# A decode block's tail on one NeuronCore: one strided store, filler matmuls, and waits merged into the matmuls

## The chip, the cores and the metric

The kernel runs on one core of one Trainium2 chip. The metric is the device time in microseconds (us) of one launch. The profile of a run covers the span from the first to the last instruction, which is shorter than the measured time; times of day in the text ("at 650.6") are us from the start of that span.

## The reference

A decode step for 4 sequences: layer norm, query projection, attention over a cache of 4096 keys and values per head, output projection and residual, then a second layer norm and an MLP with the activation h·tanh(softplus(h)).

```python
# x: (4, 1, 640); k_cache, v_cache: (4, 32, 4096, 128); all bf16
q = layernorm(x) @ wq                                   # 32 heads of 128
p = softmax(q . k_cache * 128**-0.5)
h = x + (p . v_cache) @ wo                              # wo: (4096, 640)
y = h + act(layernorm(h) @ w1 + b1) @ w2                # w1: (640, 1728), w2: (1728, 640)
```

The caches are 268 MB of the 283 MB that are read.

## The kernel before

Each engine has its own program, and they meet through semaphores. 16 K tiles and 16 V tiles go through three SBUF slots; VectorE multiplies K by the query, TensorE folds and makes the PV products. Once the last K tile is used up, its slot takes the weights wo and w1, another slot takes w2. All that the change touches is the tail: what TensorE does from the last PV product on.

```python
def need(self, *keys):                 # cut to what matters
    ...
    if sem in self.take:               # semaphores that count from zero again each loop
        self.eng.wait_ge(h, d).then_inc(h, -d)   # a wait instruction of its own, which subtracts
    elif self.live:
        self.eng.wait_ge(h, n)         # can be carried by the next instruction

def pe_tail():                         # cut
    def wo_mm(k):                      # 40 matmuls: weights 128x128 from wo, moving 4 columns
        pe.need(("wo", k), ("a", k))
        for j in range(G):
            for c in range(DC):
                w = wo_sb[:, k, j, :].rearrange("p (m c) -> p c m", c=DC)[:, c, :]  # step 5
                mm(y_ps[:, c, :], w, a_t[:, k, j, :], ...)
    wo_mm(0); o_mm(NT - 1); l_mm(hg); wo_mm(1); a_mm(hg)
    ...                                # two matmuls that clear PSUM
    wo_mm(2); wo_mm(3)
    pe.need("st")                      # sums for the second layer norm, in fp32
    ...
    pe.need("cen")
    for c0, c1 in zip(W1S, W1S[1:]):   # two parts: 42 and 28 matmuls
        pe.need(("w1", c0))
        if c1 == DC:                   # bias, in fp32
            ...
        for j in [FM] + list(range(FM)):
            for c in range(c0, c1):
                w = w1_sb[:, c, 0 : FM * P].rearrange("p (f j) -> p j f", j=FM)[:, j, :]  # step 13
                mm(h1_ps[...], w, cen[:, c, :], ...)
    pe.need("h_lo")                    # adds h: 40 small matmuls
    ...
    pe.need("act")
    def w2_mm(j):                      # 4 matmuls, one per 32-column group; weights act: 4 columns
        for k in range(CG):
            mm(y2_ps[k * QD : k * QD + N, :], act[0:rows, j, :], w2_sb[:, j, cs], ...)

for q in range(CG):                    # SyncE: the result, four rows of 320 B each time
    load(sp, out_rows[:, q * OC : (q + 1) * OC], o_bf[q * QD : q * QD + N, :], ("out", q), "OUT")
```

The softmax here doesn't subtract the row's maximum and nothing guards it: scores larger than these inputs give would overflow.

## Time and profile before

| what | number |
|---|---|
| time, median of 4 runs | 669.49 us (669.01 to 669.72) |
| span of the profiled run | 667.44 us |
| last V tile lands, last PV product starts | 637.07, 637.21 |
| fourth wo load lands | 650.37 |
| w1's first part lands, second part | 653.66, 656.09 |
| w2's three parts land | 658.67, 661.06, 661.86 |

The page of the kernel before gives, in 40 slices, the TensorE clock that was granted and the busy share of the DMA queues, in tenths:

```profile
span 667.4 us, 5166 instructions
...
PEclk9668787879759796869557887878766878788875
DMA  9999999999999999999999999999999999999995
```

The DMA row says that the queues are 90% busy or more in every slice but the last; a change behind the last V tile (637.07) can win or lose only in the last 30 us. The windows of the kernel before show stages of that tail. The columns are the window, its length, then for PE, PEld (weight loads), DVE, ACT and POOL the busy time and the number of instructions, and at the end the granted clock, the DMA share and GB/s:

```profile
642.40:644.10 1.70, 1.70 (x45) 1.68 (x41) 0.00 (x0) 1.56 (x2) 0.00 (x0) 1.00 1.01 422
649.50:650.60 1.10, 0.01 (x1) 0.00 (x0) 0.00 (x0) 0.00 (x0) 0.00 (x0) 0.50 0.96 399
650.60:652.40 1.80, 1.73 (x40) 1.68 (x40) 0.00 (x0) 0.00 (x0) 0.00 (x0) 0.50 0.98 407
654.00:656.50 2.50, 2.50 (x41) 2.48 (x42) 0.57 (x5) 1.58 (x2) 0.00 (x0) 0.50 1.04 370
661.20:663.40 2.20, 2.19 (x56) 1.62 (x56) 0.00 (x0) 0.00 (x0) 0.00 (x0) 0.50 0.00 1
```

The first and third lines are the first and the fourth part of wo: 40 matmuls in the same 1.7 us, once at clock 1.00 and once at 0.50. The second line is TensorE's one long idle stretch behind the last V tile and before the activation chain, 1.1 us. The fourth is w1's first part, the fifth w2. The timeline of the kernel before (start, length, engine, line, operation, out<-in, count, and in brackets the idle time before it) shows the end of the chain:

```profile
650.66 1.73 PE L657 MATMUL y_ps<-a_t,slotB 128*128 128x4 bf16 x40 [1.15 <-PEq L44]
652.66 0.62 PE L657 MATMUL misc<-st,ones_d 128*128 128x20 f32 x2 [0.27 <-DVE st L562]
653.53 0.18 DVE L582 TENSOR_TENSOR cen<-st,mu 128x20 bf16<-128x20 f32 x1
654.00 2.73 PE L657 MATMUL red<-cen,slotB 128*64 128x4 bf16 x42 [0.30 <-PEq L44]
656.59 0.66 PE L657 MATMUL red<-b1s,ident_f 128*128 128x56 f32 x2
657.18 1.93 PE L657 MATMUL red<-cen,slotB 128*64 128x4 bf16 x28
660.69 0.22 DVE L646 SCALAR_TENSOR_TENSOR act<-tb,hm 128x56 bf16<-128x56 f32 x1
661.21 0.30 PE L657 MATMUL red<-w_tail,act 64*4 64x160 bf16 x4 [1.35 <-PEq L44]
663.44 0.32 DVE L653 CAST o_bf<-red 128x160 bf16<-128x160 f32 x1 [2.53 <-PE red L657]
663.79 1.33 SPq L239 DMA_DIRECT2D out_dram<-o_bf  x4
```

Each line waits for the one above it. The fourth wo part waits for its load (the releaser "PEq" is TensorE's own wait instruction, which hides the DMA behind it). The activations are ready at 660.91 and the first w2 matmul starts at 661.21, 0.3 us later. The four stores take 1.33 us to issue.

### The profile page before, as it was taken

How to read it: one execution, taken by the hardware profiler on the slowest of the kernel's cores; microseconds unless marked ns; L12 is line 12 of the kernel's file. 1: busy time of each engine (PE TensorE's matmuls, PEld its weight loads, DVE VectorE, ACT ScalarE, POOL GpSimd, SP SyncE). 2: the span in 40 equal slices, each digit the busy share in tenths (PEclk: the TensorE clock that was granted, in tenths of full speed). 3: DMA queues.
4: the chain of work that ended last, by engine and by line, in shares of the span. 5: the costliest groups of instructions: out<-in, count | busy, mean ns of one | idle time of the engine just before them, and what ended most of it. 6: DMA issues, size and time to landing. Idle time of an engine off the chain costs nothing. (4 is left out here: it accounts for less than half of the span.)

```text
span 667.4 us, 5166 instructions
## 1 busy us (share of the span) xinstructions
PE 394.1 (59%) x2729; PEld 79.4 (12%) x1769; DVE 406.5 (61%) x250; ACT 41.0 (6%) x157; POOL 2.6 (0%) x14
## 2 busy tenths in 40 slices
PE   0855748456327585847308395848426575847576
PEld 0700100101101010101100010100110010010155
DVE  1068988295058788666128798768208798849412
ACT  0200000000000010000000000000000000000011
POOL 1000000000000000000000000000000000000000
PEclk9668787879759796869557887878766878788875
DMA  9999999999999999999999999999999999999995
GB/s 378 437 440 440 433 420 409 441 440 437 429 436 436 436 436 424 424 440 436 432 432 440 436 432 432 416 440 436 433 432 436 440 436 433 428 425 440 428 396 198
DMA packets 6405, 283.55 MB, mean 425 GB/s; under 512 B 948, under 2 KB 1016, under 8 KB 1528
## 3 DMA queue, kind: packets, MB, share of 16 engines
q1 hardware_dynamic: 6160, 283.35, 98.5%
q8 instruction: 10, 0.16, 0.1%
q10 hardware_dynamic: 232, 0.01, 0.0%
q14 instruction: 3, 0.02, 0.0%
HBM read 283.35 MB, written 0.01 MB: 425 GB/s over the span
## 5 line engine op out<-in xcount | busy, mean ns | idle before, releaser
L466 DVE TENSOR_TENSOR slotA<-slotA,q_bc 128x8192 bf16<-128x8192 bf16 x32 | 140.7, 4416 | 110.9 <-DMA slotA<-in_A_k_cache_dram 110.7
L466 DVE TENSOR_TENSOR slotB<-slotB,q_bc 128x8192 bf16<-128x8192 bf16 x32 | 140.7, 4416 | 16.3 <-DMA slotB<-in_A_k_cache_dram 16.3
L667 PE MATMUL red<-slotA,ident 128*128 128x512 bf16 x480 | 141.0, 459 | 0.0
L477 DVE TENSOR_REDUCE s_f<-red 128x64 f32<-128x1024 f32 x64 | 78.1, 1220 | 96.9 <-PE red L667 96.8
L667 PE MATMUL red<-slotB,ident 128*128 128x512 bf16 x480 | 123.3, 415 | 0.0
L657 PE MATMUL red<-slotA,ident 128*128 128x512 bf16 x32 | 14.2, 445 | 119.3 <-PEq L44 119.3
L657 PE MATMUL pv<-slotC,e 128*32 128x512 bf16 x768 | 52.4, 434 | 42.7 <-PEq L44 42.7
L657 PE MATMUL red<-slotB,ident 128*128 128x512 bf16 x32 | 14.1, 441 | 87.0 <-PEq L44 87.0
L348 ACT ACTIVATE ex<-s_f 128x64 bf16<-128x64 f32 x64 | 16.4, 256 | 502.3 <-DVE s_f L477 502.3
L491 DVE TENSOR_TENSOR e<-ex,hmask 128x512 bf16<-128x512 bf16 x64 | 39.8, 682 | 0.0
L657 PEld LDWEIGHTS pv<-slotC,e 128*32 128x32 bf16 x768 | 22.5, 108 | 103.0 <-issue 89.4
L657 PEld LDWEIGHTS red<-slotA,ident 128*128 128x128 bf16 x32 | 3.2, 98 | 200.7 <-issue 200.6
L657 PEld LDWEIGHTS red<-slotB,ident 128*128 128x128 bf16 x32 | 3.2, 98 | 165.1 <-issue 165.1
L657 PEld LDWEIGHTS o_ps<-pv_sb,selo 128*32 128x32 f32 x128 | 12.7, 109 | 59.1 <-issue 59.1
L657 PE MATMUL o_ps<-pv_sb,selo 128*32 128x128 f32 x128 | 17.0, 276 | 0.0
L657 PE MATMUL pv<-slotA,e 128*32 128x512 bf16 x256 | 14.5, 380 | 0.9 <-PEq L44 0.9
L358 ACT COPY pv_sb<-pv 128x512 f32<-128x512 f32 x16 | 9.4, 585 | 75.7 <-PE pv L657 75.7
L348 ACT ACTIVATION_READ_ACCUMULATOR ex<-s_f 128x1 f32 x64 | 11.9, 186 | 0.0
L657 PE MATMUL red<-q_all,sel 32*128 32x128 bf16 x128 | 10.8, 280 | 0.8 <-PEq L44 0.8
L657 PEld LDWEIGHTS red<-q_all,sel 32*128 32x128 bf16 x128 | 10.6, 128 | 1.2 <-issue 1.2
L516 DVE RECIPROCAL rl<-misc 32x1 f32<-32x1 f32 x4 | 0.6, 150 | 16.2 <-PE misc L657 16.2
L657 PEld LDWEIGHTS pv<-slotA,e 128*32 128x32 bf16 x256 | 7.0, 97 | 22.1 <-issue 16.5
(93 smaller groups left out, 74.0 us busy)
## 6 DMA issues: line engine op xcount, KB each, us to landing
slotC<-in_A_wq_dram SPq DMA_DIRECT2D x1, 5120.0 KB, 15.1
slotB<-in_A_wo_dram SPq DMA_DIRECT2D x4, 1280.0 KB, 19.1
slotB<-in_B_w_dram SPq DMA_DIRECT2D x1, 1296.0 KB, 26.8
slotA<-in_B_w_dram SPq DMA_DIRECT2D x1, 960.0 KB, 30.3
slotB<-in_B_w_dram SPq DMA_DIRECT2D x1, 864.0 KB, 28.8
slotA<-in_B_w_dram SPq DMA_DIRECT2D x1, 800.0 KB, 32.0
slotA<-in_B_w_dram SPq DMA_DIRECT2D x1, 320.0 KB, 30.2
slotC<-in_A_v_cache_dram SPq DMA_DIRECT2D x12, 44.9
```

Source lines behind the costliest of these rows:

```text
L348: lambda: a.activation(out=ex[:, sl], in_=s_f[:, sl], func=ACT.Exp, scale=SCALE, accum_out=rs[:, b, s : s + 1],),
L358: lambda: a.copy(out=pv_sb[:, :, :].rearrange("p r d -> p (r d)"), in_=pv[:, :]),
L466: lambda: v.tensor_tensor(out=t, in0=t, in1=q_bc[:, hg, b, :].unsqueeze(1).to_broadcast([P, RS, Dh]), op=ALU.mult,),
L477: lambda: v.tensor_reduce(out=s_f[:, s * RS : (s + 1) * RS], in_=red[:, k : k + 2, :].rearrange("p k (r c) -> p (k r) c", c=CW), axis=AX.X ...
L491: lambda: v.tensor_tensor(out=e[:, sl, :], in0=ex[:, sl].unsqueeze(2).to_broadcast([P, RS, G]), in1=hmask[:, :].unsqueeze(1).to_broadcast( ...
L516: dv.do(lambda: v.reciprocal(out=rl[:, :], in_=l_ps), ("rl", hg), DV)
L657: lambda: nc.tensor.matmul(out_, lhsT=lhsT, rhs=rhs, start=start, stop=stop, skip_group_check=skip),
L667: return t.add_instruction(mybir.InstMatmult(name=nc.get_next_instruction_name(), engine=mybir.EngineType.PE, ins=[t.lower_ap(rhs), t.lowe ...
```

## The change

Its intent: TensorE's clock falls to half in the tail, so fill its gaps with matmuls that compute nothing and keep the clock up; let the first matmul behind a wait carry the wait; give the result in one store instead of four. For the store, the result's 16 rows have to lie at an even step over the partitions, so h and the activations get 32-column weights, 28 of the columns zero, which puts the rows eight partitions apart.

```diff
+    def freeze(self):                       # from here on the taken semaphores are no longer reset
+        self.base = dict(self.seen)
-            if sem in self.take:
+            if sem in self.take and self.base is None:
...
+                low = self.base.get(sem, 0) if sem in self.take else 0
+                self.eng.wait_ge(h, n - low)
...
+    spread = sb("spread", (P, 2 * DC + FC, N, ROW), BF16, tail, topA)   # zeroed; ROW = 8
+    h_hi, h_lo, act = (...)                 # every eighth column of it
...
-        for q in range(CG):
-            load(sp, out_rows[:, q * OC : (q + 1) * OC], o_bf[q * QD : q * QD + N, :], ...)
+        load(sp, out_rows.rearrange("b (k o) -> k b o", k=CG), o_bf[0:P:ROW, :], "out", "OUT")
...
+    def keep_busy(n):                       # fillers: 128x128 weights, 512 moving columns
+        for k in range(n):
+            (mm_same if k else mm)(red[:, 3, :], ident[:, :], slot["C"][:, 0:512], True, True)
...
+        pe.freeze()
         wo_mm(0)
+        keep_busy(4)
         o_mm(NT - 1)
         l_mm(hg)
         wo_mm(1)
+        keep_busy(4)
         a_mm(hg)
...
         wo_mm(2)
+        keep_busy(6)
         wo_mm(3)
...                                          # the norm sums
+        keep_busy(4)
         pe.need("cen")
         for c0, c1 in zip(W1S, W1S[1:]):
-            pe.need(("w1", c0))
             if c1 == DC:
                 ...                          # bias
+                keep_busy(3)
+            pe.need(("w1", c0))
...                                          # h, now with 32-column weights
+        keep_busy(3)
         pe.need("act")
...                                          # w2, now with 32-column weights
+            if j0 == 0:
+                keep_busy(4)
```

More of the change, by code (lines that the diff above doesn't have):

```diff
@@ L27, in restart @@
         self.log = []
+        self.base = None
+    def freeze(self):
+        self.base = dict(self.seen)
     def need(self, *keys):
@@ L45, in need @@
             elif self.live:
-                self.eng.wait_ge(h, n)
+                low = self.base.get(sem, 0) if sem in self.take else 0
+                self.eng.wait_ge(h, n - low)
     def do(self, fn, mark=None, sem=None, by=1):
@@ L192 @@
     b1s = sb("b1s", (P, FC, N), FP32, tail, topA)
-    h_hi = sb("h_hi", (P, DC, N), BF16, tail, topA)
-    h_lo = sb("h_lo", (P, DC, N), BF16, tail, topA)
+    ROW = QD // N
+    spread = sb("spread", (P, 2 * DC + FC, N, ROW), BF16, tail, topA)
+    h_hi, h_lo, act = (
+        spread[:, j0:j1, :, :] for j0, j1 in ((0, DC), (DC, 2 * DC), (2 * DC, 2 * DC + FC))
+    )
     h1 = sb("h1", (P, FC, N), FP32, tail, topA)
@@ L200 @@
     hm2 = sb("hm2", (P, FC, N), FP32, tail, topA)
-    act = sb("act", (P, FC, N), BF16, tail, topA)
     o_bf = sb("o_bf", (P, OC), BF16, tail, topA)
@@ L286, in sync_prog @@
         sp.need("o_bf")
-        for q in range(CG):
-            load(
-                sp, out_rows[:, q * OC : (q + 1) * OC], o_bf[q * QD : q * QD + N, :],
-                ("out", q), "OUT",
-            )
-        sp.need(("out", CG - 1))
+        load(
+            sp, out_rows.rearrange("b (k o) -> k b o", k=CG), o_bf[0:P:ROW, :], "out", "OUT",
+        )
+        sp.need("out")
     def pool_prog():
@@ L311, in pool_prog @@
         po.do(lambda: g.memset(ones_d[:, :], 1.0 / D), "ones_d", "PO")
+        po.do(lambda: g.memset(spread[:, :, :, :], 0.0), "spread", "PO")
         po.do(lambda: g.memset(zeros[:, :], 0.0), "zeros", "PO")
@@ L600, in dve_prog @@
         )
-        dv.do(lambda: v.tensor_copy(out=h_hi[:, :, :], in_=st[:, 0, :, :]), "h_hi", DV)
+        dv.do(lambda: v.tensor_copy(out=h_hi[:, :, :, 0], in_=st[:, 0, :, :]), "h_hi", DV)
         dv.need("std2", "b1b")
@@ L613, in dve_prog @@
             lambda: v.tensor_tensor(
-                out=h_lo[:, :, :], in0=st[:, 0, :, :], in1=h_hi[:, :, :], op=ALU.subtract
+                out=h_lo[:, :, :, 0], in0=st[:, 0, :, :], in1=h_hi[:, :, :, 0], op=ALU.subtract
             ),
@@ L646, in dve_prog @@
             lambda: v.scalar_tensor_tensor(
-                out=act[:, :, :], in0=tb3[:, :, :], scalar=-0.5, in1=hm2[:, :, :],
+                out=act[:, :, :, 0], in0=tb3[:, :, :], scalar=-0.5, in1=hm2[:, :, :],
                 op0=ALU.add, op1=ALU.mult,
@@ L846, in pe_tail @@
                     mm(
-                        y2_ps[k * QD : k * QD + N, :].rearrange("b (m c) -> b c m", c=DC)[:, c, :],
-                        part[:, c, :], ident[:, k * QD : (k + 1) * QD], False, False,
+                        y2_ps[k * QD : (k + 1) * QD, :].rearrange("b (m c) -> b c m", c=DC)[:, c, :],
+                        part[:, c, :, :].rearrange("p n r -> p (n r)"), ident[:, k * QD : (k + 1) * QD], False, False,
                     )
+        keep_busy(3)
         pe.need("act")
@@ L857, in w2_mm @@
                 mm(
-                    y2_ps[k * QD : k * QD + N, :], act[0:rows, j, :],
+                    y2_ps[k * QD : (k + 1) * QD, :],
+                    act[0:rows, j, :, :].rearrange("p n r -> p (n r)"),
                     w2_sb[:, j, cs] if j < FM else w2_tail[0:FT, cs], False, j == FM - 1,
```

## The prediction

> **What bounds the kernel now.** Until the last V tile it streams the caches: the page shows DMA 90% busy or more in all but the last of 40 slices, 425 GB/s. The change touches only what comes after that tile lands (637.0 of a 667.4 us span), so at most 30 us are in play.
>
> In that tail (timeline, windows) TensorE runs without a gap from 637.2 to 649.5: the last PV product 5.2 us, then wo parts of 40 matmuls at 40 ns each, o, l, a. The only real gap is 649.5 to 650.6, for the fourth wo load (landed 650.35). Then a chain: wo part 4 (1.7 us), norm sums, centring (653.7), w1 (60 ns per matmul, to 659.1), activation chain on VectorE (to 660.9), 56 w2 matmuls (661.2 to 663.4, 133 ns per four), copy, four stores issued 0.3 us apart (663.8 to 665.1), the last landing at 666.0, and 1.4 us of fixed end.
>
> **Clock.** The granted clock is 1.00 from 640.5 to 647.4 and 0.50 after. It changes only at steps of 3.41 us, as the Trainium skill, "TensorE: Matmul & The Clock Gate", Part 1, says of its activity window. I counted array work per window (columns times used share of the array): windows at 0.44 of full rate or more stayed fast, those at 0.31 or less fell, and from the slow clock 0.38 was not enough. Is a fast clock worth having? The wo matmuls take 40 ns at 1.00 and at 0.50 alike; the a matmuls take 60 ns at 1.00, as w1's do at 0.50. So wo and w1 are bound by weight loads that do not follow the clock. Only w2 (160 columns at half rate are the 133 ns), the fp32 sums and the bias would gain: about 0.9 + 0.5 us.
>
> **Change, costed.**
> - Store: three issues of 0.3 us leave the chain's end: -0.95 us.
> - Waits: separate wait instructions cost 0.25 us from release to first weight load (act 660.91 to 661.18). Merged: about -0.2 us where still exposed.
> - Fillers: 28 matmuls of 128x512, 0.213 us each fast, 0.427 us slow (the fold matmuls show both), mostly not in gaps. 14 stand before wo part 4, where the gap is 1.1 us. Four beside 3.5 us of small matmuls give about 0.33 of full rate: I expect the clock to fall at 647 to 651 anyway. Then groups 1 to 3 cost 0.9 + 1.3 + 2.6 less the gap: +3.5; the group behind the sums +1.35; behind the bias +1.3; behind h_lo mostly hidden in the 1.9 us activation chain, +0.6; inside w2 +1.7.
> - 32-column padded weights for h and act: w2 stays 133 ns per four; they raise counted activity, so the clock may rise during w2: -0.5 to -1.
>
> Sum: about +6.5 us. If the fillers do hold the clock at 1.00, only about +1.3 us.
>
> **Prediction:** 675.8 us, range 670.5 to 678.5; faster by over 2% 0.01, within 2% 0.97, slower by over 2% 0.02.
>
> **What would show it.** Windows: from the end of the last PV product to wo part 4 grows from 8.3 to 11 to 12.5 us; wo still 40 ns and w1 still 60 ns per matmul at any clock; clock 0.50 over most of w1; one store, landing about 1.1 us after its issue; cen ready over 1 us before the w1 matmuls; TensorE no longer idle before wo part 4.
>
> **What would make it wrong.** Fillers holding the clock at 1.00 (then near 670.6); w1's weight loads following the clock after all, which would save up to 2.5 us and make the change a gain (near 667.5); 32-column weight loads slowing the h products enough to delay w2; another phase of the clock's window.

## The result, and the profile after

| | before | after |
|---|---|---|
| median, 4 runs each | 669.49 us | 675.38 us (674.19 to 675.62) |
| span of the profiled run | 667.44 us | 672.40 us |

The changed kernel is 5.9 us slower; the ratio is 1.0085 with a 95% interval of 1.0068 to 1.0103. Ratios here and below are the mean time of one kernel's fast runs over that of the other's of the same rounds, so not quite the ratio of the medians quoted. The profiled run of the changed kernel is its fastest (674.19), so its profile shows 5.0 us of the loss.

The page of the changed kernel, clock and DMA:

```profile
span 672.4 us, 5177 instructions
...
PEclk9668887879758697968658796868658887879786
DMA  9999999999999999999999999999999999999992
```

The windows of the changed kernel, in the same columns:

```profile
642.50:644.30 1.80, 1.76 (x44) 1.70 (x41) 0.00 (x0) 1.66 (x2) 0.00 (x0) 1.00 1.04 438
651.10:653.40 2.30, 2.06 (x5) 0.15 (x1) 0.00 (x0) 0.00 (x0) 0.00 (x0) 0.50 1.02 410
653.50:655.20 1.70, 1.70 (x41) 1.64 (x39) 0.00 (x0) 0.00 (x0) 0.00 (x0) 0.80 1.05 362
655.80:656.90 1.10, 1.04 (x6) 0.24 (x3) 0.80 (x6) 0.18 (x1) 0.00 (x0) 1.00 1.05 418
656.90:659.40 2.50, 2.50 (x43) 2.46 (x43) 0.44 (x3) 1.40 (x2) 0.00 (x0) 0.64 0.79 308
659.70:661.30 1.60, 1.25 (x4) 0.25 (x3) 0.00 (x0) 0.00 (x0) 0.00 (x0) 0.50 0.14 54
666.60:668.10 1.50, 1.50 (x8) 0.05 (x1) 0.00 (x0) 0.00 (x0) 0.00 (x0) 0.59 0.00 0
668.10:668.80 0.70, 0.70 (x29) 0.47 (x28) 0.00 (x0) 0.00 (x0) 0.00 (x0) 1.00 0.00 0
```

The second line is the group of six fillers before the fourth wo part, at clock 0.50: 2.3 us that TensorE does nothing useful in, where it had 1.1 us idle. (The trace holds five records of the six: the first one's matmul is missing, though its weight load is there at 650.92.) The wo and w1 lines (third, fifth) take what they took before, 1.7 us for 40 and 2.5 us for 42, at whatever clock. The last line is the second half of w2 at clock 1.00, 28 matmuls in 0.67 us where they took about 0.9 us before. That and the first of the fp32 norm sums (0.40 us for 0.62, below) are the places seen here where the clock pays. The timeline of the changed kernel, for the lines shown of before:

```profile
651.34 2.34 PE L674 MATMUL red<-slotC,ident 128*128 128x512 bf16 x5 [0.24 <-issue]
...
653.47 1.76 PE L664 MATMUL y_ps<-a_t,slotB 128*128 128x4 bf16 x40
655.50 0.40 PE L664 MATMUL misc<-st,ones_d 128*128 128x20 f32 x2 [0.27 <-DVE st L569]
656.15 0.18 DVE L589 TENSOR_TENSOR cen<-st,mu 128x20 bf16<-128x20 f32 x1
656.18 0.81 PE L674 MATMUL red<-slotC,ident 128*128 128x512 bf16 x3
656.92 2.65 PE L664 MATMUL red<-cen,slotB 128*64 128x4 bf16 x42
659.44 0.66 PE L664 MATMUL red<-b1s,ident_f 128*128 128x56 f32 x2
661.30 1.94 PE L664 MATMUL red<-cen,slotB 128*64 128x4 bf16 x28 [0.36 <-issue]
664.82 0.41 DVE L653 SCALAR_TENSOR_TENSOR spread<-tb,hm 128x56 bf16<-128x56 f32 x1
665.37 0.32 PE L664 MATMUL red<-w_tail,spread 64*32 64x160 bf16 x4
668.85 0.32 DVE L660 CAST o_bf<-red 128x160 bf16<-128x160 f32 x1 [3.62 <-PE red L664]
669.20 0.69 SPq L247 DMA_DIRECT2D out_dram<-o_bf  x1
```

The fourth wo part starts at 653.47 instead of 650.66; its load had landed at 650.46, so nothing but the fillers holds it. The centred h is ready at 656.33, and fillers run until w1 can start at 656.92. VectorE's write of the activations into every eighth column takes 0.41 us for 0.22. The store's one issue takes 0.69 us, about twice the 0.33 us that each of the four took before.

The same stages side by side, each from the start of its first matmul to that of the next stage's, with what the prediction gave:

| stage | before | after | difference | predicted |
|---|---|---|---|---|
| first to fourth wo part | 8.25 | 10.97 | +2.72 | +3.5 |
| fourth wo part to w1 | 3.34 | 3.45 | +0.11 | +1.35, less a merged wait |
| w1's first part to its second (bias between) | 3.18 | 4.38 | +1.20 | +1.3 |
| w1's second part to w2 | 4.03 | 4.07 | +0.04 | +0.6, less a merged wait |
| w2 to the copy of the result | 2.23 | 3.48 | +1.25 | +0.7 to +1.2 |
| copy to the end | 4.00 | 3.55 | -0.45 | -0.95 |

Up to the first wo part 0.09 us are lost; the sum is the 4.96 us between the spans. TensorE's clock was 1.00 from 640.5 to 650.8, 0.50 to 654.2, 1.00 again to 657.6, 0.50 to 667.8.

### The profile page after: what moved, and what is told of

Same layout as the page of the kernel before. It is cut to its first block, busy times and chain, and to the rows that moved or that the text cites. A ratio compares the mean times of both kernels' runs of the same rounds, so it can differ in the third digit from the quotient of the medians.

```text
span 672.4 us, 5177 instructions
## 1 busy us (share of the span) xinstructions
PE 402.8 (60%) x2751; PEld 78.9 (12%) x1776; DVE 406.8 (61%) x250; ACT 41.0 (6%) x157; POOL 3.3 (0%) x15
## 5 line engine op out<-in xcount | busy, mean ns | idle before, releaser
L674 PE MATMUL red<-slotA,ident 128*128 128x512 bf16 x480 | 139.2, 454 | 0.0
L674 PE MATMUL red<-slotB,ident 128*128 128x512 bf16 x480 | 127.0, 424 | 0.0
L664 PE MATMUL red<-slotA,ident 128*128 128x512 bf16 x32 | 14.3, 448 | 119.7 <-PEq L49 119.7
L664 PE MATMUL red<-slotB,ident 128*128 128x512 bf16 x32 | 14.1, 440 | 87.9 <-PEq L49 87.9
L664 PE MATMUL red<-q_all,sel 32*128 32x128 bf16 x128 | 10.9, 281 | 0.8 <-PEq L49 0.8
L664 PE MATMUL red<-slotC,lnT 128*32 128x512 bf16 x40 | 3.8, 558 | 9.9 <-PEq L49 9.9
```

Of the source, the lines that this page charges most:

```text
L664: lambda: nc.tensor.matmul(out_, lhsT=lhsT, rhs=rhs, start=start, stop=stop, skip_group_check=skip),
L674: return t.add_instruction(mybir.InstMatmult(name=nc.get_next_instruction_name(), engine=mybir.EngineType.PE, ins=[t.lower_ap(rhs), t.lowe ...
```

## The experiments

The theory (T1): the fillers cost the time because they stand where TensorE has no gap, and everything else in the change is a small gain. A rival (T2): the padded weights, strided writes or merged waits carry part of the loss. Another (T3): the fillers buy something through the clock, so that holding the clock properly would make them pay.

### no_fill

```diff
 # the changed kernel; every keep_busy(n) taken out
```

> The changed kernel with all 28 filler matmuls taken out; single store, merged waits, padded weights stay. Theory T1 (the fillers cost time because they stand where TensorE has no gap; the rest is a small gain): about 668.8 us, i.e. 0.4 to 1.0 us under the kernel before (store -0.45 us as the traces of before and after show, merged waits -0.2 to -0.4). Rival T2 (the padded weights, the strided VectorE writes or the merged waits cost part of the loss): above 670.5 us. Rival T3 (the fillers buy something by the clock): slower in the w2 stage than the changed kernel by 0.4 us or more, at a granted clock of 0.50; T1 expects that too, but no more than that.

The timeline of no_fill, for the fourth wo part, the start of w2 and the copy:

```profile
650.41 1.76 PE L664 MATMUL y_ps<-a_t,slotB 128*128 128x4 bf16 x40 [0.46 <-DMA slotB<-in_A_wo_dram]
660.83 0.32 PE L664 MATMUL red<-w_tail,spread 64*32 64x160 bf16 x4 [1.24 <-DVE spread L653]
663.06 0.33 DVE L660 CAST o_bf<-red 128x160 bf16<-128x160 f32 x1 [2.28 <-PE red L664]
```

Measured: 668.62 us against 669.31 of the kernel before on the same chip, ratio 0.9989 (0.9976 to 1.0003). T1's number. Without its fillers the change is a gain of 0.7 us if anything (the interval just holds 1). T2 is out. On T3: from the start of w2 to the copy no_fill takes 2.22 us; the changed kernel takes 3.48 us, of which 1.6 us are the filler group and what stands around it (first filler's weights at 666.54, next w2 matmul at 668.13), so 1.9 us of its own. The fillers buy 0.3 us there, a little less than expected, and pay 1.6 us for it. The prediction had put that gain down to the padded weights. But here, with the padding and no fillers, the clock stays at 0.50 from 648.43 to the end, as it does in nofill_4st from 650.30, while in fill_only, without the padding, it rises during w2 (at 669.47): the fillers raise it.

### fill_only and fill_early

```diff
 # the kernel before
+ keep_busy(4) / (4) / (6)      behind wo parts 1, 2, 3            (both)
+ keep_busy(4) / (3) / (3) / (4) behind sums, bias, h, first w2    (fill_only)
```

> The kernel before with the 28 fillers at the same places and nothing else of the change. T1: about 675.9 us, 6 to 6.5 us over before, spread of 1 us or so by where the clock falls. T2: under 673.

> The kernel before with only the 14 fillers in front of the fourth wo part. T1: +2.7 to +3.6 us over before (672.2 to 673.1), from the end of the last PV product to the first matmul of the fourth wo part 10.9 to 11.8 us for 8.3. If the fillers mostly fitted into gaps: within 1 us of before.

Measured: fill_only 676.07 us, ratio to before 1.0087 (1.0073 to 1.0100); fill_early 671.96 us, ratio 1.0040 (1.0027 to 1.0054). The fillers alone make the whole loss: fill_only's ratio and the changed kernel's (1.0085) can't be told apart, though its median is 0.7 us higher. The 14 in front of the fourth wo part make 2.65 us of it, a little under the 2.7 that was expected at least. The stretch expected to grow to 10.9 us or more grew to 10.43 us only (642.95 to 653.38): in that run the clock stayed at 1.00 until 652.0, so that nearly half of the third group still ran fast, while the last PV product had taken 0.66 us longer, because the clock had come up 1.2 us later.

fill_only's runs fall into two groups, 674.1 (2 runs) and 676.1 (3 runs). Its profiled run is of the longer group. The windows of fill_only, from the norm sums to w1:

```profile
655.50:656.30 0.80, 0.74 (x4) 0.74 (x5) 0.27 (x3) 0.00 (x0) 0.00 (x0) 0.50 1.03 400
656.30:658.20 1.90, 1.90 (x6) 0.21 (x2) 1.10 (x9) 1.13 (x2) 0.00 (x0) 0.50 0.98 393
```

The second line is the group of four fillers at clock 0.50: 1.9 us, where the profile of the changed kernel (its fastest run) needs 1.1 us for the sums' end and the group together at 1.00. From the sums to w1 it is 2.68 us here and 1.42 us there. So the same stretch differs by 1.3 us between a profile in which the clock is at 0.50 there and one in which it is at 1.00. That this is what parts the two groups, which lie 2.0 us apart, is not shown: no run of fill_only's shorter group was profiled, and the mean clock doesn't sort the runs (0.806 and 0.808 in the short ones of fill_only against 0.786 to 0.791 in the long; 0.786 to 0.791 in the short ones of the changed kernel against 0.789 to 0.805 in the long).

### nofill_4st

```diff
 # no_fill
- load(sp, out_rows.rearrange("b (k o) -> k b o", k=CG), o_bf[0:P:ROW, :], "out", "OUT")
+ for q in range(CG):
+     load(sp, out_rows[:, q * OC : (q + 1) * OC], o_bf[q * QD : (q + 1) * QD : ROW, :], ("out", q), "OUT")
```

> As no_fill, but with the four stores of before. T1: 0.45 us slower than no_fill, since the traces show 1.79 us from the result's copy to the seen landing for the one store and 2.24 us for the four; so about 669.3. My prediction had 0.95 us for the store; that value would make it about 0.95 us slower than no_fill.

Measured: 670.37 us, 1.75 us more than no_fill and 1.06 us more than before (ratio 1.0015, 1.0001 to 1.0028). Neither value came. The reason shows in the stores. First nofill_4st, four stores of four rows eight partitions apart, then store_2q (below), four stores of four adjacent rows; the three numbers are the shortest, median and longest issue in ns:

```profile
L247 SPq DMA_DIRECT2D out_dram<-o_bf x4: 578/591/735, 663.7 to 665.7; - x4
```

```profile
L239 SPq DMA_DIRECT2D out_dram<-o_bf x2: 267/308/348, 663.8 to 664.2; - x2
L239 ACTq DMA_DIRECT2D out_dram<-o_bf x2: 302/312/321, 663.8 to 664.1; - x2
```

An issue of rows that are eight partitions apart takes 0.58 to 0.74 us, of adjacent rows 0.27 to 0.35 us, for the same four rows of 320 B. The number of rows counts for little: 16 strided rows took 0.69 us. So this was no clean undoing of the store, and it shows what the single store's stride costs: by these numbers about 0.35 us (0.69 less 0.33) of the 1.0 us that three issues fewer would have saved.

### waits_only

```diff
 # the kernel before, with freeze() and wait_ge(h, n - low) of the change, and
         for c0, c1 in zip(W1S, W1S[1:]):
-            pe.need(("w1", c0))
             ...                              # bias
+            pe.need(("w1", c0))
```

> The kernel before with only the merged tail waits (and the bias matmul ahead of the wait for the second w1 part), no fillers, no padding, four stores. T1: 0.3 to 0.45 us under before, so 668.9 to 669.0: the fourth wo part starts 0.25 us sooner after its load, w2 starts about 0.15 us sooner after its activations. If the merge did nothing by itself, within 0.1 us of before.

Measured: 668.85 us against 669.41, 0.56 us less; ratio 0.9990 (0.9977 to 1.0004), so in the total not clear of the noise. Whether the fourth wo part follows its load sooner can't be seen in this profile: the load landed at 649.69, while TensorE came only at 650.64. It can be seen in no_fill, which has the same waits: 0.04 us after the landing (650.37) instead of 0.29. From w1's second part to w2 it takes 3.79 us for 4.03: the merged waits give 0.24 us there. no_fill has the same waits and takes 3.98 us: the strided write of the activations gives 0.19 us of it back. So the padding costs nearly what the merge gains at that place; my prediction did not have that term.

### clock_hold

```diff
 # the changed kernel
-        keep_busy(4)      # behind the sums
+        keep_busy(20)
-                keep_busy(3)      # behind the bias
+                keep_busy(20)
```

> The changed kernel with 20 fillers instead of 4 ahead of w1 and 20 instead of 3 between its parts, so that the granted clock is 1.00 over most of w1. The time is not the point (about 10 to 15 us slower). My reading that w1's weight loads do not follow the clock: 59 to 60 ns per w1 matmul at clock 1.00. Rival (they follow it, and steady fillers would pay): about 40 ns or less at clock 1.00.

Measured: 682.83 us, one run, 13.4 us over the kernel before and 7.5 us over the changed one. The windows of clock_hold over w1's two parts:

```profile
662.50:665.00 2.50, 2.50 (x42) 2.48 (x42) 0.00 (x0) 0.00 (x0) 0.00 (x0) 1.00 0.00 0
669.70:671.60 1.90, 1.90 (x32) 1.85 (x33) 0.00 (x0) 0.00 (x0) 0.00 (x0) 1.00 0.00 0
```

The granted clock is 1.00 throughout and both parts take the 2.5 and 1.9 us that they take at 0.50 in the kernel before; the steps from one matmul to the next lie between 58 and 68 ns, most at 59 to 61, in both. T3 is out for w1: no number of fillers would make it faster.

### contig

```diff
 # waits_only; columns of wo and w1 assigned so that a weight load reads 128 adjacent elements
-  w = wo_sb[:, k, j, :].rearrange("p (m c) -> p c m", c=DC)[:, c, :]                # step 5
+  w = wo_sb[:, k, j, c * P : (c + 1) * P]
-  w = w1_sb[:, c, 0 : FM * P].rearrange("p (f j) -> p j f", j=FM)[:, j, :]          # step 13
+  w = w1_sb[:, c, j * P : (j + 1) * P]
 # rows of w1 and w2, the bias and the h products laid out to match
```

> waits_only with the columns of wo and w1 assigned so that a weight load reads 128 adjacent elements (steps of 5 and 13 elements before); w2's rows and the bias are laid out to match, arithmetic is the same. If the step of the read sets the 40 and 60 ns per matmul and not the granted clock: both go to one lower value (40 ns or less) at the same clock of 0.50, the w1 parts lose 1.4 us or more, and the total is 667.5 to 668.2, the last w2 loads (landed at 661.8) being the next limit. If the granted clock or the sequencer sets it: 40 and 60 ns stay, and the time is that of waits_only.

The windows of contig, the first wo part and w1's first part:

```profile
643.34:644.35 1.01, 1.01 (x44) 1.01 (x40) 0.00 (x0) 0.88 (x2) 0.00 (x0) 1.00 1.04 436
653.80:655.10 1.30, 1.30 (x42) 1.28 (x42) 0.24 (x3) 1.15 (x1) 0.00 (x0) 0.50 1.07 308
```

42 w1 matmuls in 1.3 us instead of 2.5, at the same clock of 0.50. The step from one matmul to the next is 25 ns for wo at clock 1.00, and 26 to 27 ns for wo and w1 at 0.50. So it is the step of the weight read that set 40 ns (step 5) and 60 ns (step 13); with adjacent elements a slight dependence on the clock appears.

And yet the total was 669.03 us (ratio to before 0.9992, 0.9979 to 1.0006), no better than waits_only (668.85); the expected 667.5 to 668.2 was missed. The timeline of contig shows where the 2 us went:

```profile
659.29 0.97 PE L665 MATMUL red<-slotA,act 128*4 128x160 bf16 x24
661.27 1.30 PE L665 MATMUL red<-slotA,act 128*4 128x160 bf16 x28 [1.01 <-DMA slotA<-in_B_w_dram]
...
662.13 0.10 PEld L665 LDWEIGHTS red<-slotA,act 128*4 128x4 bf16 x8 [0.37 <-DMA slotA<-in_B_w_dram]
```

w2 starts at 659.06, 2.15 us earlier than before, and then waits for its second and third loads, which landed at 661.22 and 662.09. The tail is then bound by its last loads. The rest of the miss lies outside the profiled span: contig's measured times exceed its spans by 1.7 to 2.7 us, waits_only's by 1.8 to 1.9 us; why is open.

### store_2q, waits_2q and contig_2q

```diff
 # SyncE issues stores 0 and 1 of the kernel before, ScalarE stores 2 and 3
+        ac.need("o_bf")
+        for q in (2, 3):
+            load(ac, out_rows[:, q * OC : (q + 1) * OC], o_bf[q * QD : q * QD + N, :], ("out", q), "OUT2")
```

> The kernel before with its four stores of adjacent rows, two issued by the sync engine and two by the scalar engine at the same time. If a store's issue of about 0.3 us each is what stands at the end of the chain: two of four leave it, 0.6 us under before (668.7). If issues of the two engines are served one after the other: no gain.

> The kernel before with the merged waits and the four stores issued two each by the sync and the scalar engine; no fillers, no padding. The two gains measured one at a time were 0.56 and 0.59 us. If they lie on the same chain and add: 668.2 to 668.4. If they overlap: 668.8.

> contig with the two-engine store. If the last w2 load (landed at 662.09 in contig) now sets the end, the store gain of about 0.5 us is kept and the total is 668.3 to 668.6, no better than waits_2q although w1 and wo run 2 us faster. If compute still set it, it would be 667 or less.

Measured: store_2q (on the kernel before) 668.82 us against 669.41, ratio 0.9994 (0.9980 to 1.0007), so 0.6 us by the medians but not clear of the noise; waits_2q (on waits_only) 668.14 us against 669.54, ratio 0.9981 (0.9968 to 0.9995); contig_2q 668.47 us, ratio 0.9983 (0.9970 to 0.9997). The two engines do issue side by side: the issues end 0.66 us after they start instead of 1.33. waits_2q has what is useful of the change, without fillers, padding or stride, and is the fastest version here, 7 us under the changed kernel and 0.2% under the kernel before, with an interval that does not hold 1. contig_2q is as expected no better: the last load sets its end.

### after_again

```diff
 # the changed kernel, unchanged
```

> The changed kernel once more, for a second profile. Its first profile was the fastest of its runs (674.19, the others 675.4 to 675.6), with the clock back at 1.00 from 654.2 to 657.6. Expected: 675.4, and then the stretch from the norm sums to the first w1 matmul 2.4 to 2.7 us instead of 1.42, because the clock stayed at 0.50 there; or, at 674.2, the same as in the first profile.

Measured: 674.03, 674.09, 675.44 and 676.01 us; ratio 1.0085 (1.0069 to 1.0100). The profiled run was again one of the shorter ones (674.03), with the clock at 1.00 from 654.0 to 657.4 and 1.42 us from the sums to w1, as in the first profile. Over both sets the changed kernel has three runs at 674.0 to 674.2 and five at 675.4 to 676.0. That the longer ones are those in which the clock does not rise at 654 is argued, not shown: none of them was profiled.

## Why the prediction was right

- **The total.** 675.8 predicted, 675.38 measured, within the range. The sign, and that the fillers make nearly all of it, was right: no_fill and fill_only show it from both sides. That the number came so close is partly luck: for the run that was profiled the sum of +6.5 us is 1.5 us too high, and misses of opposite sign (below) meet in it. Two of the signs that it named stayed short there: 10.9 us from the last PV product to the fourth wo part for 11 to 12.5, and the centred h was ready 0.6 us before w1, not over 1 us.
- **No gaps to fill.** Right. Before the fourth wo part 14 fillers met 1.1 us of idle time and cost 2.72 us in the profile and 2.65 us alone (fill_early). The group behind h fitted into the 1.9 us activation chain: +0.04 us in the changed kernel, 0.00 in fill_only (4.03 us there and in the kernel before). The prediction had put 0.6 us down for it. That is what a real gap looks like: TensorE waits there for a chain on other engines that is longer than the fillers.
- **The clock.** Its uselessness for wo and w1 was right, and clock_hold and contig settle it: at clock 1.00 w1 takes the same time, and with adjacent weights it takes half of it at 0.50. My forecast of when the clock would move was only half right. It fell at 650.8 as forecast, but rose again from 654.2 to 657.6. By my count (columns times used share of the array) the window before that rise held 0.32 of full rate, 0.38 with the filler whose record is missing, and windows of 0.38 had not been enough in the kernel before; in fill_only a window of 0.33 with all its fillers on record (666.05 to 669.47) was enough. So the count is not the right measure; what decides the clock stays open.
- **Terms that were off.** The rise of the clock made the group behind the sums cost 0.11 us net in the profiled run instead of +1.35 less a merged wait; in fill_only, where it did not rise, it cost 1.34 us (2.68 for 1.34). The groups before the fourth wo part cost 0.8 us less than predicted. From the last matmul in front of a group to the first behind it 0.88, 0.66 and 1.22 us were added, for 0.9, 1.3 and 1.5 (2.6 less the gap of 1.1): the second ran fast (its four took 0.95 us of the 1.3 that I had put down as a mean) and covered 0.3 us in which TensorE had waited for VectorE (646.71 to 647.04 in the kernel before), and the third met 1.3 us between two matmuls (649.33 to 650.66), not 1.1. What a filler costs depends on where the clock's windows fall. And the fast clock during w2 came, but from the fillers and not from the padded weights (no_fill, fill_only).
- **The store.** Predicted -0.95, measured -0.45 us: I costed the one store as one issue of before, 0.3 us, and it took 0.69 us because its rows are eight partitions apart (nofill_4st: 0.58 to 0.74 us each). The issue saved 0.64 us, and the landing, 1.07 us behind the end of the issue for 0.88 before, gave 0.2 us of it back.
- **A term that was missing.** The padding's strided write, 0.41 for 0.22 us on VectorE, in the critical chain; it takes back most of the 0.24 us of the merged wait there.
- **Why the spread grew.** The kernel before repeats within 0.9 us over all its runs, the changed one scatters over 2 us. In the kernels without fillers the fourth wo part started at 650.25 to 650.84 in all six of them whose wo was as before (in three it waited for its load, which landed at 650.31 to 650.37; in three TensorE came 0.7 to 1.1 us after the landing), though the last PV product took between 5.20 and 6.48 us depending on when the clock rose. The fillers used up that slack, and their own length doubles with the clock (0.213 to 0.427 us). That this makes the spread is argued; no run was made for it.

On the Trainium skill: "TensorE: Matmul & The Clock Gate", Part 1, has the clock at half or full rate, moved at windows of about 3.4 us. These traces agree: granted clock 0.50 and 1.00 only, changes at multiples of 3.41 us. Its advice to keep TensorE busy for throughput (section "Why this matters for your kernels") holds for matmuls that stream many columns (w2's four-matmul group goes from 133 to 70 ns); it does not hold for those of 4 columns here. "DMA: Bandwidth & Descriptors", section "Issuing engines are not separate DMA queues", says that issuing from several engines saves only the sequencer's issue time; store_2q agrees, with 0.67 us saved in its trace, which is a lot where the issue stands alone at the end of a kernel.

## What to carry to other kernels

A filler is free only where the engine waits for something longer than the filler; find that in the idle times of the engine, not in its clock, and count the filler at its slow length. Before paying for a faster clock, look for one group of instructions that ran at both clocks: if its time is the same, the clock is not what it waits for, and the cause (here the step of the weight read) has to be found first. And cost a new DMA by its own access pattern: one strided store took as long to issue as two plain ones.

## What the Trainium skill lacked or had wrong

- "TensorE: Matmul & The Clock Gate", section "LDWEIGHTS (loading the stationary operand)", gives a weight load's time by its number of columns alone (columns over 1.2; by that formula an estimate of 107 ns for 128). That is not far from the 96 and 104 ns that contig's trace has for one load of wo and w1 with adjacent elements (medians), but it has no term for the step: 131 ns at a step of 5 elements, 158 ns at 13. Nor is it the pace: load-and-matmul pairs with 4 moving columns follow each other every 25 to 27, 40 and 60 ns. Its section on weight-path modes allows steps up to 1,024 elements for the fast load without a cost for the step, and what the skill says elsewhere of strided reads has no time for a weight load.
- The same page does not say that small matmuls behind strided weight loads are deaf to the clock: 40 and 60 ns at granted clock 0.50 and 1.00 alike.
- The same page says that the clock rises after a busy window, but not how much work makes a window busy: five 512-column matmuls among small ones raised it in fill_only (0.33 of full rate by my count) where 0.38 had not in the kernel before.
- "DMA: Bandwidth & Descriptors" has nothing on what a partition step costs at issue: 0.27 to 0.35 us for four adjacent rows, 0.58 to 0.74 us for four rows eight partitions apart, 0.69 us for 16 of them.
